# Six places of a written-out instruction order in a fused attention and MLP kernel

## The chip, the cores and the metric

The kernel runs on one core of a Trainium2 chip. The core has five engines that work through separate instruction lists: TensorE (PE in the profile, with its weight loads as PEld), VectorE (DVE), ScalarE (ACT), GpSimd (POOL) and SyncE (SP, which here only issues DMAs). They wait for each other through semaphores. The metric is the device time of one execution in microseconds; lower is better.

## The reference

Two layers, the same weights in both, act on x of shape 1 x 2048 x 512 in bfloat16:

```python
x = A_x
x = x + _A_ref(_layernorm(x, axis=-1), A_wqkv, A_wo)
x = x + _B_ref(_layernorm(x, axis=-1), B_w1, B_b1, B_w2, B_b2)
x = x + _A_ref(_layernorm(x, axis=-1), A_wqkv, A_wo)
x = x + _B_ref(_layernorm(x, axis=-1), B_w1, B_b1, B_w2, B_b2)
```

`_A_ref` is attention with 32 heads of 16 elements, where a query sees itself and the 255 keys before it: `qkv = x @ wqkv`, scores times 1/4, a softmax under that window, the sum over values, and a product with `wo`. `_B_ref` is an MLP of width 1792: `gelu(x @ w1 + b1) @ w2 + b2` with the tanh form of gelu. `_layernorm` subtracts a row's mean and divides by the root of its variance plus 1e-5.

## The kernel before

The 2048 rows are 16 tiles of 128 rows; over the two layers that makes 32 tiles (0 to 31), and 16 blocks of two tiles (0 to 15; blocks 8 to 15 are the second layer). X, all weights, the keys and values of the last blocks and the MLP's hidden rows stay in SBUF. The ten MLP jobs take two or four tiles each.

A block b runs through these steps; the name in brackets is the key of the step in the code, with b, a tile or an index behind it.

- Layer norm in front of attention (`layernorm`): statistics of a row tile on VectorE (`bs`, line 585, and `ba`, line 587), variance plus epsilon (`vp`, line 591) and the power -1/2 on POOL (`pw`, line 597), the normalised rows on VectorE (`xn`, line 607). Then a transpose: by a DMA transpose that SP issues (`tx`, line 612), or for the first four and the last tiles on TensorE (`tp`, line 619) with a copy out of PSUM (`te`, line 574 on VectorE, 576 on ACT). Numbers from 32 up belong to the layer norm in front of the MLP: `xn57` is the row tile 25 of that kind.
- Projections on TensorE, line 633: `q`, `k` (four steps of two matmuls for each half of the columns, so `q5_1.3` is block 5, second half, last step) and `v` by tile. Out of PSUM they go by `qe` (line 574 or 576), `ke` (VectorE, line 667, which also writes zeros between the heads by `parmask`) and `ve` (line 574 or 576). For each tile of V two DMAs write a copy shifted by 64 rows (`vs`, line 682).
- Attention in ten visits of a block (five in the blocks that begin a layer): scores on TensorE (`sc`, line 734), two exponentials on ACT (`ex`, line 741), 0/1 masks on VectorE or POOL (`mk`, line 762). For each half of the heads then follow the sums over values with a column of row sums (`pv`, line 784), a transpose out of PSUM (`od`, line 793), the reciprocal (`rc`, line 797), the normalisation (`nm`, line 801) and a transpose back (`ot`, line 807), all on VectorE or, for some `nm`, on POOL.
- The product with wo (`op`, line 633) and its sum into X (`rs`, line 833).
- The MLP: `m` (first product, line 633), bias on VectorE (`gb`, line 856) and gelu on ACT over two hidden chunks (`ga`, line 859), or both on ACT (`ge`, line 864); X plus b2 on POOL (`xb`, line 872); `y` (second product, 14 chunks, line 633); `ya` (line 876) adds it to X. In the second layer a tile is then stored (`out`, line 880).
- Loads: X by `ldx`, wqkv by `ldw`, w1 by `ldu`, and W2's hidden chunks in four parts, `ldz0` to `ldz3` (line 564); `ldz3` holds chunks 11 to 13.

The order of the work is written out by hand. The program adds its 3080 steps to a list, each with its engine, what it reads and writes, and the PSUM banks it takes and frees. Their numbers in the list `_ORDER` say in which order they are emitted. Each engine executes its own steps in that order. So a number that moves past steps of other engines alone changes nothing in what the engines execute. `_ALT` says which steps run on their second engine, and `_BANKS` gives the PSUM banks in the order in which they are taken.

While the steps are emitted, `_Sched.op` derives the waits: a step waits for the steps that wrote what it reads, or that still read what it writes, by the counter of their engine. DMAs use eight counters in turn, and a DMA first waits until the one eight places before it, on the same counter, has landed. SP executes its waits and issues one after the other, so that a DMA whose data are not ready holds all that stand behind it.

Of the kernel before, what the change touches and what calls it, by code (L numbers as in the profile page):

```python
# [19 lines left out]
class _Sched:  # L20
# [148 lines left out]
    61, 26, 59, 106, 20, 39, 62, 104, 28, 63, 40, 32, 64, 67, 38, 65, 107, 105, 68, 108, 66, 49, 27, 109, 69, 47, 29,  # L169
    48, 54, 5, 80, 70, 113, 81, 110, 82, 6, 114, 324, 111, 115, 71, 55, 72, 112, 73, 152, 83, 74, 126, 116, 84, 127,  # L170
    117, 128, 118, 119, 153, 150, 129, 120, 194, 130, 97, 196, 98, 31, 99, 42, 85, 195, 151, 100, 154, 366, 101, 10,
    86, 11, 367, 87, 322, 75, 103, 155, 76, 90, 521, 102, 88, 368, 91, 77, 325, 156, 78, 323, 92, 89, 79, 326, 198,
    327, 131, 199, 93, 132, 12, 94, 157, 133, 134, 200, 136, 135, 202, 137, 96, 203, 138, 139, 158, 25, 95, 121, 140,
    204, 216, 159, 201, 122, 143, 217, 144, 205, 123, 145, 197, 124, 218, 328, 146, 519, 207, 147, 125, 141, 219, 212,
    208, 213, 170, 171, 172, 214, 330, 329, 43, 370, 209, 206, 173, 210, 371, 174, 175, 160, 161, 162, 372, 163, 176,
    520, 148, 215, 177, 164, 374, 149, 373, 220, 211, 376, 331, 44, 165, 221, 166, 375, 180, 167, 168, 178, 522, 169,
    222, 379, 523, 223, 181, 524, 381, 142, 230, 225, 226, 224, 45, 231, 380, 182, 377, 179, 183, 227, 232, 184, 233,
    382, 384, 234, 185, 228, 385, 342, 229, 343, 51, 332, 378, 333, 237, 386, 187, 52, 337, 369, 334, 235, 335, 50,
    344, 238, 394, 387, 338, 396, 388, 345, 188, 236, 189, 383, 339, 346, 239, 336, 190, 240, 389, 395, 241, 527, 191,
    242, 641, 398, 347, 400, 390, 348, 340, 349, 350, 399, 352, 243, 359, 525, 244, 351, 402, 353, 403, 192, 391, 354,  # L180
    360, 341, 392, 361, 355, 404, 356, 407, 362, 409, 357, 363, 248, 249, 53, 262, 250, 263, 408, 412, 393, 193, 252,
    253, 414, 264, 528, 245, 411, 246, 254, 255, 247, 256, 410, 413, 427, 257, 526, 563, 259, 565, 397, 278, 260, 279,
    186, 261, 428, 564, 422, 416, 405, 275, 365, 276, 423, 272, 287, 281, 284, 290, 273, 566, 288, 277, 285, 282, 280,
# [5 lines left out]
    437, 537, 592, 650, 538, 556, 557, 558, 584, 593, 559, 595, 438, 651, 585, 439, 596, 652, 440, 586, 896, 597, 653,  # L189
    441, 560, 599, 587, 654, 600, 659, 660, 655, 656, 601, 588, 661, 598, 604, 589, 898, 662, 605, 456, 457, 899, 442,  # L190
    487, 458, 443, 606, 657, 444, 445, 452, 663, 453, 594, 658, 609, 446, 610, 459, 454, 466, 897, 467, 447, 449, 900,
    611, 450, 603, 607, 463, 469, 901, 478, 451, 460, 464, 612, 472, 664, 481, 461, 479, 470, 590, 468, 482, 465, 473,
# [91 lines left out]
    2300, 2581, 2291, 2284, 2285, 2301, 2484, 2580, 2304, 2562, 2302, 2485, 2305, 2292, 2286, 2294, 2287, 2572, 2486,  # L284
    2295, 2279, 2280, 2563, 2296, 2288, 2306, 2492, 2493, 2256, 2554, 2281, 2314, 2494, 2315, 2278, 2282, 2582, 2495,
    2307, 2496, 2309, 2267, 2316, 2297, 2317, 2568, 2310, 2320, 2283, 2573, 2321, 2322, 2298, 2323, 2324, 2325, 2293,
# [4 lines left out]
    2350, 2601, 2768, 2351, 2518, 2769, 2519, 2520, 2600, 2424, 2425, 2421, 2770, 2426, 2602, 2521, 2771, 2578, 2772,  # L291
    2603, 2522, 2773, 2523, 2524, 2525, 2427, 2774, 2604, 2537, 2544, 2605, 2538, 2545, 2526, 2539, 2505, 2775, 2540,
    2606, 2546, 2428, 2776, 2541, 2547, 2430, 2778, 2607, 2608, 2548, 2506, 2609, 2610, 2777, 2612, 2611, 2781, 2613,
    2543, 2782, 2614, 2617, 2780, 2615, 2354, 2504, 2355, 2618, 2616, 2356, 2783, 2357, 2786, 2619, 2371, 2422, 2787,
    2358, 2359, 2620, 2372, 2784, 2335, 2621, 2373, 2788, 2360, 2622, 2429, 2796, 2374, 2797, 2375, 2423, 2790, 2361,
    2362, 2625, 2363, 2364, 2623, 2798, 2376, 2789, 2800, 2779, 2626, 2365, 2801, 2366, 2785, 2799, 2367, 2377, 2368,
    2791, 2802, 2624, 2370, 2804, 2792, 2700, 2378, 2805, 2379, 2380, 2381, 2382, 2806, 2793, 2803, 2809, 2383, 2384,
    2810, 2654, 2794, 2385, 2655, 2643, 2656, 2811, 2657, 2807, 2814, 2658, 2644, 2815, 2645, 2812, 2646, 2649, 2813,
    2647, 2650, 2816, 2651, 2652, 2808, 2923, 2627, 2924, 2818, 2638, 2628, 2817, 2675, 2629, 2925, 2795, 2630, 2819,
# [4 lines left out]
    2833, 2703, 2704, 2834, 2752, 2753, 2705, 2836, 2933, 2706, 2707, 2708, 2835, 2837, 2709, 2710, 2932, 2838, 2839,  # L304
    2936, 2711, 2754, 2938, 2840, 2755, 2935, 2756, 2934, 2757, 2841, 2712, 2937, 2713, 2714, 2758, 2715, 2941, 1971,
    2759, 2942, 2842, 2760, 2751, 2550, 2761, 2762, 2735, 2943, 2542, 2763, 2951, 1954, 2736, 2952, 2737, 2944, 2764,
    2843, 2765, 2738, 2766, 2739, 2953, 2740, 2955, 2939, 2549, 2718, 2940, 2957, 2945, 2741, 2742, 2743, 2744, 2956,
    2745, 2746, 2747, 2748, 2719, 2749, 2958, 2720, 2959, 2946, 2750, 2961, 2906, 2767, 2960, 2847, 2947, 2851, 2848,
    2963, 2852, 2721, 2854, 2853, 2969, 2954, 2722, 2971, 2962, 2855, 2849, 2723, 2861, 2948, 2724, 2970, 2725, 2856,
    2949, 2844, 2726, 2727, 2845, 2972, 2964, 2973, 2728, 2846, 2966, 2729, 2950, 2730, 2862, 2731, 2965, 2863, 2880,  # L310
    2865, 2732, 2858, 2881, 2866, 2968, 2733, 2859, 2967, 2984, 2860, 2979, 2352, 2974, 2386, 2850, 2857, 2907, 2975,
# [636 lines left out]
```

## Time and profile before

| | |
|---|---|
| time, median of 3 runs | 460.92 us (460.57 to 461.63) |
| profiled execution, its own time | 459.81 us |
| its span | 458.0 us, mean granted TensorE clock 0.992 |
| TensorE busy | 421.5 us (92%) |
| weight loads | 230.7 us (50%) |
| VectorE busy | 345.7 us (75%) |
| ScalarE busy | 389.7 us (85%) |
| POOL busy | 201.3 us (44%) |
| share of the chain that ended last | PE 60%, ACT 17%, DVE 13%, DMA 4%, SP 2% |

The busy shares are means over the whole span; matmuls are pipelined, so a busy TensorE is not one at its peak. The chain is followed back from the last instruction: at each step to what released it, or to the instruction before it on its engine. In a timeline, a line gives the start in us from the span's start, the duration, engine, line and operation, what it writes and reads, shapes, how many instructions were joined, and in brackets the idle time before it with what ended it.

These DMA issues are the ones that the change moves or moves past (start of the issue, its duration, and landing where the trace has one, in us):

| step | issue | lasts | landed |
|---|---|---|---|
| vs6_0 | 43.46 | 0.47 | |
| ldz3 | 43.98 | 0.58 | 49.55 |
| vs5_1 | 44.62 | 0.53 | 49.75 |
| tx9 | 45.19 | 3.45 | 50.93 |
| tx8 | 48.69 | 1.26 | 51.53 |
| vs4_1 | 49.99 | 0.73 | 52.24 |
| out1 | 414.11 | 0.58 | 416.06 |
| vs31_1 | 414.74 | 0.47 | 416.88 |
| vs30_0 | 415.25 | 0.60 | 417.33 |
| out0 | 415.88 | 0.59 | 419.81 |
| tx61 | 416.51 | 2.55 | 420.33 |
| vs31_0 | 419.11 | 0.58 | |

### The profile page before, as it was taken

The page shows a single profiled execution, that of the slowest core. Times are in us where ns is not written, and L with a number is a line of the kernel's source. Part 1 is how long each engine was busy: PE and PEld are TensorE (multiplying, and loading weights), DVE is VectorE, ACT ScalarE, POOL GpSimd, SP SyncE. Part 2 cuts the span into 40 slices and gives each one's busy share as a digit, 9 for nine tenths or more (in the row PEclk, how much of TensorE's full clock was granted, in tenths as well). Part 3 has the DMA queues.
Part 4 walks back from the last instruction along what each step waited for, and adds up shares of the span by engine and source line. Part 5 has one row for each costly group of instructions (what it writes and reads, how often), then busy time and mean ns, then how long its engine had stood idle before and what let it go on. Part 6 is the DMA issues. An engine that isn't in the chain of part 4 may idle for free.

```text
span 458.0 us, 16828 instructions
## 1 busy us (share of the span) xinstructions
PE 421.5 (92%) x7505; PEld 230.7 (50%) x7579; DVE 345.7 (75%) x640; ACT 389.7 (85%) x463; POOL 201.3 (44%) x225
## 2 busy tenths in 40 slices
PE   7998999986789997899999998999999999999996
PEld 4555646543434553445445454455554554444573
DVE  6999699787773878986698688857987497755762
ACT  2998979988799999789999988999889988898642
POOL 4272614054336145351855563564652444524230
PEclk9999999998899999999999999999999999999999
DMA  8687311202300103210032022010422003003110
GB/s 236 192 216 171 71 32 26 43 9 35 82 4 1 24 15 66 58 26 0 3 61 44 0 59 35 10 43 1 74 45 53 1 4 89 3 1 91 36 47 24
DMA packets 47972, 23.25 MB, mean 51 GB/s; under 512 B 33180, under 2 KB 47900, under 8 KB 47900
## 3 DMA queue, kind: packets, MB, share of 16 engines
q1 hardware_dynamic: 47900, 22.17, 21.8%
q8 instruction: 60, 0.98, 1.0%
q14 instruction: 12, 0.10, 0.1%
HBM read 8.00 MB, written 2.10 MB: 22 GB/s over the span
## 4 chain that ended last, share of the span: by engine, by line
PE 60%; ACT 17%; DVE 13%; DMA 4%; issue 3%; SPq 2%; POOL 1%; DVEq 0%
PE ps L633 44%; ACT E L741 11%; PE ps L784 8%; PE ps L734 8%; ACT gT L864 3%; DVE E L762 2%; DVE OD L793 2%; ACT gT L859 2%; DMA xnTB<-xn 2%; DVE xn L607 2%; DVE gT L856 1%; DMA xnTA<-xn 1%; DVE Va L574 1%; DVE OT L807 1%; DVE X L876 1%
## 5 line engine op out<-in xcount | busy, mean ns | idle before, releaser
L741 ACT ACTIVATE E<-ps 128x1024 bf16<-128x1024 f32 x300 | 283.8, 1035 | 40.1 <-PE ps L734 39.4
L762 POOL TENSOR_TENSOR E<-E,mask 128x512 bf16<-128x512 bf16 (+2 forms) x104 | 114.6, 1115 | 100.4 <-ACT E L741 100.1
L633 PE MATMUL ps<-xnTB,W_sb 128*128 128x512 bf16 (+1 forms) x541 | 110.8, 336 | 4.9 <-issue 1.4
L633 PE MATMUL ps<-W_sb,gT 128*128 128x512 bf16 x418 | 110.9, 380 | 3.8 <-issue 2.5
L633 PE MATMUL ps<-xnTA,Wqkv_sb 128*128 128x256 bf16 x512 | 75.2, 274 | 2.3 <-DMA xnTA<-xn 1.2
L633 PEld LDWEIGHTS ps<-xnTB,W_sb 128*128 128x128 bf16 x560 | 51.3, 98 | 47.9 <-issue 5.5
L762 DVE TENSOR_TENSOR E<-E,mask 128x768 bf16<-128x768 bf16 (+2 forms) x132 | 63.5, 498 | 10.7 <-ACT E L741 10.6
L734 PE MATMUL ps<-QT,KT 32*128 32x128 bf16 (+3 forms) x1920 | 61.5, 232 | 10.7 <-ACT E L741 3.9
L734 PEld LDWEIGHTS ps<-QT,KT 32*128 32x128 bf16 x1920 | 28.9, 93 | 64.2 <-ACT E L741 38.5
L633 PEld LDWEIGHTS ps<-W_sb,gT 128*128 128x128 bf16 x448 | 39.9, 98 | 40.5 <-issue 2.7
L793 DVE STREAM_TRANSPOSE OD<-ps 128x1024 f32<-128x1024 f32 x32 | 39.8, 1244 | 25.9 <-PE ps L784 25.8
L633 PEld LDWEIGHTS ps<-xnTA,Wqkv_sb 128*128 128x128 bf16 x512 | 46.3, 98 | 25.7 <-issue 5.5
L864 ACT ACTIVATE gT<-ps,b1T 128x512 bf16<-128x512 f32 (+1 forms) x80 | 43.4, 610 | 11.5 <-PE ps L633 11.4
L784 PE MATMUL ps<-E,Va 64*17 64x128 bf16 (+3 forms) x1920 | 44.2, 233 | 4.6 <-DVE E L762 1.9
L801 POOL TENSOR_TENSOR Nb<-OD,Rc 128x512 bf16<-128x512 f32 x17 | 18.3, 1076 | 64.4 <-DVE Rc L797 64.4
L667 DVE TENSOR_TENSOR KT<-ps,parmask 128x1024 bf16<-128x1024 f32 x32 | 38.7, 1210 | 10.2 <-PE ps L633 9.9
L872 POOL TENSOR_TENSOR Xb<-X,b2all 128x512 f32<-128x512 bf16 x32 | 37.9, 1193 | 19.1 <-DVE X L876 11.7
L856 DVE TENSOR_SCALAR gT<-ps,b1T 128x512 bf16<-128x512 f32 (+1 forms) x60 | 37.3, 632 | 11.4 <-PE ps L633 10.3
L784 PE MATMUL ps<-E,Vs 64*17 64x128 bf16 (+3 forms) x1920 | 44.9, 233 | 0.0
L585 DVE BATCH_NORM_STATS2 stat<-X 128x6 f32<-128x512 bf16 x64 | 42.6, 679 | 2.9 <-DMA X<-in_A_x_dram 2.5
L784 PEld LDWEIGHTS ps<-E,Va 64*17 64x17 bf16 x1920 | 37.2, 85 | 14.0 <-issue 9.0
L633 PE MATMUL ps<-Wo_sb,OT 128*128 128x512 bf16 x118 | 37.4, 387 | 2.8 <-DVE E L762 1.2
(51 smaller groups left out, 363.1 us busy)
## 6 DMA issues: line engine op xcount, KB each, us to landing
Vs<-Va SPq DMA_DIRECT2D x64, 68.0 KB, 2.5
W_sb<-in_B_w_dram SPq DMA_DIRECT2D x4, 512.0 KB, 6.0
out_dram<-X SPq DMA_DIRECT2D x16, 128.0 KB, 1.9
X<-in_A_x_dram SPq DMA_DIRECT2D x3, 512.0 KB, 6.3
Wqkv_sb<-in_A_wqkv_dram SPq DMA_DIRECT2D x4, 256.0 KB, 6.0
W_sb<-in_B_w_dram SPq DMA_DIRECT2D x1, 768.0 KB, 5.8
W_sb<-in_B_w_dram SPq DMA_DIRECT2D x2, 384.0 KB, 5.1
Wqkv_sb<-in_A_wqkv_dram SPq DMA_DIRECT2D x1, 512.0 KB, 7.0
```

Of the source, the lines that this page charges most:

```text
L585: add("dve", lambda e, B, t=t, k6=k6: e.bn_stats(stat6[:, k6, :], X[:, t, :]), reads=["X%d" % t], writes=["st%d" % k6], key="bs%d" % (k + j))
L633: r = e.matmul(ps[:, B[g][0], cols], lhsT, rhs, start=st, stop=sp)
L667: add("dve", lambda e, B, g=g, i=i: e.tensor_tensor(out=KT[:, kb, 2 * i : 2 * i + 2].rearrange("p c m a q -> p a (c m) q"), in0=ps[:, B[g] ...
L734: x = e.matmul(ps[:, bk[r], o : o + n], KT[rows, kb, c, m].rearrange("p a q -> p (a q)"), QT[rows, c, q : q + n], start=True, stop=True)
L741: add("act", lambda e, B, g_=g_, gi=gi: e.activation(E[:, 2 * gi : 2 * gi + 2, e0 : e0 + 512], ps[:, B[g_][0] : B[g_][0] + 2, :], AF.Exp, ...
L762: fn = lambda e, B: e.tensor_tensor(out=Ew, in0=Ew, in1=Mw, op=ALU.mult)
L784: x = e.matmul(ps[32 * r : 32 * r + VW, B[g][par], c % 2 * 2 * P + lo : c % 2 * 2 * P + hi], V[rows, (2 * b + m // 2) % VR, c * HC + 2 * r ...
L793: add("dve", lambda e, B: e.transpose(OD[:, s].rearrange("p a c q -> p (a c q)"), ps[:, B[g][0] : B[g][0] + 2, :]), reads=["ps:" + g], wri ...
L801: return e.tensor_tensor(out=Nb[:, s, :].rearrange("p (k a d) -> p a k d", a=2, d=Dh), in0=sums[:, :, :, 0:Dh], in1=rc[:, :, :, None].to_b ...
L856: add("dve", lambda e, B, g=g, fc=fc: e.tensor_scalar(out=gT[:, fc, c0 : c0 + M], in0=ps[:, B[g][0], 0:M], scalar1=b1T[:, fc : fc + 1], sc ...
L864: add("act", lambda e, B, g=g, fc=fc: e.activation(gT[:, fc, c0 : c0 + M], ps[:, B[g][0], 0:M], AF.Gelu_apprx_tanh, bias=b1T[:, fc : fc + ...
L872: add("pool", lambda e, B, t=t, xs=xs: e.tensor_tensor(out=Xb[:, xs, :], in0=X[:, t, :], in1=b2all[:], op=ALU.add), reads=["X%d" % t, "b2a ...
```

## The change

Only `_ORDER` differs. Most of the numbers that move there pass steps of other engines alone. Read engine by engine, ACT and POOL execute the same lists as before, the PSUM banks are taken in the same order, and this is what differs:

- VectorE, at the start: the list `bs7, te2, bs5, ke0_0, ba5, bs4, ke1_0, ba4` (numbers 324, 112, 152, 84, 153, 150, 130, 151) becomes `te2, bs7, ke0_0, bs5, ba5, ke1_0, bs4, ba4`. So the copy of a transposed row tile and the first key evictions of blocks 0 and 1 stand in front of a statistic each.
- SP: `ldz3, vs5_1, tx9, tx8` (53, 193, 528, 526) becomes `vs5_1, tx9, tx8, ldz3`.
- TensorE: `q5_1.3` (657) goes in front of `m1_4.0, m1_4.1, m1_0.0, m1_0.1` (456, 457, 442, 443).
- VectorE: `xn57, ot13_1` (2505, 2606) becomes `ot13_1, xn57`; the transpose of block 13's output stands in front of the normalised rows of tile 25.
- SP: `out1, vs31_1, vs30_0, out0, tx61, vs31_0` (1971, 2550, 2542, 1954, 2843, 2549) becomes `vs31_1, vs30_0, tx61, vs31_0, out1, out0`.

The eight DMA counters go by place, so the DMAs in the two stretches of SP change counters among themselves.

```diff
...
-    48, 54, 5, 80, 70, 113, 81, 110, 82, 6, 114, 324, 111, 115, 71, 55, 72, 112, 73, 152, 83, 74, 126, 116, 84, 127,
-    117, 128, 118, 119, 153, 150, 129, 120, 194, 130, 97, 196, 98, 31, 99, 42, 85, 195, 151, 100, 154, 366, 101, 10,
+    48, 54, 5, 80, 70, 113, 81, 110, 82, 6, 114, 111, 115, 71, 55, 72, 112, 324, 73, 83, 84, 74, 126, 116, 152, 127,
+    117, 128, 118, 42, 119, 153, 129, 130, 150, 120, 194, 97, 196, 98, 31, 99, 85, 195, 151, 100, 154, 366, 101, 10,
...
-    360, 341, 392, 361, 355, 404, 356, 407, 362, 409, 357, 363, 248, 249, 53, 262, 250, 263, 408, 412, 393, 193, 252,
-    253, 414, 264, 528, 245, 411, 246, 254, 255, 247, 256, 410, 413, 427, 257, 526, 563, 259, 565, 397, 278, 260, 279,
+    360, 341, 392, 361, 355, 404, 356, 407, 362, 409, 357, 363, 248, 249, 262, 250, 263, 408, 412, 393, 193, 252, 253,
+    414, 264, 528, 245, 411, 246, 254, 255, 247, 256, 410, 413, 427, 257, 526, 563, 259, 565, 397, 278, 260, 53, 279,
...
-    441, 560, 599, 587, 654, 600, 659, 660, 655, 656, 601, 588, 661, 598, 604, 589, 898, 662, 605, 456, 457, 899, 442,
-    487, 458, 443, 606, 657, 444, 445, 452, 663, 453, 594, 658, 609, 446, 610, 459, 454, 466, 897, 467, 447, 449, 900,
+    441, 560, 599, 587, 654, 600, 659, 660, 655, 656, 601, 588, 661, 598, 604, 589, 898, 662, 605, 657, 456, 457, 899,
+    442, 487, 458, 443, 606, 444, 445, 452, 663, 453, 594, 658, 609, 446, 610, 459, 454, 466, 897, 467, 447, 449, 900,
...
-    2603, 2522, 2773, 2523, 2524, 2525, 2427, 2774, 2604, 2537, 2544, 2605, 2538, 2545, 2526, 2539, 2505, 2775, 2540,
-    2606, 2546, 2428, 2776, 2541, 2547, 2430, 2778, 2607, 2608, 2548, 2506, 2609, 2610, 2777, 2612, 2611, 2781, 2613,
+    2603, 2522, 2773, 2523, 2524, 2525, 2427, 2774, 2604, 2537, 2544, 2605, 2538, 2545, 2526, 2539, 2606, 2505, 2775,
+    2540, 2546, 2428, 2776, 2541, 2547, 2430, 2778, 2607, 2608, 2548, 2506, 2609, 2610, 2777, 2612, 2611, 2781, 2613,
...
-    2936, 2711, 2754, 2938, 2840, 2755, 2935, 2756, 2934, 2757, 2841, 2712, 2937, 2713, 2714, 2758, 2715, 2941, 1971,
-    2759, 2942, 2842, 2760, 2751, 2550, 2761, 2762, 2735, 2943, 2542, 2763, 2951, 1954, 2736, 2952, 2737, 2944, 2764,
-    2843, 2765, 2738, 2766, 2739, 2953, 2740, 2955, 2939, 2549, 2718, 2940, 2957, 2945, 2741, 2742, 2743, 2744, 2956,
+    2936, 2711, 2754, 2938, 2840, 2755, 2935, 2756, 2934, 2757, 2841, 2712, 2937, 2713, 2714, 2758, 2715, 2941, 2759,
+    2942, 2842, 2760, 2751, 2550, 2761, 2762, 2735, 2943, 2542, 2763, 2951, 2736, 2952, 2737, 2944, 2764, 2843, 2765,
+    2738, 2766, 2739, 2953, 2740, 2955, 2939, 2549, 2718, 2940, 1971, 2957, 1954, 2945, 2741, 2742, 2743, 2744, 2956,
...
```

18 rows, old and new, of the table _ORDER are left out of this document.

## The prediction

> **What bounds the kernel now.** I read the page first (engines, chain), then the chain in order of time, then the timeline of each engine around the six places. All durations are from the one profiled execution: span 458.0, its own time 459.81, so 1.8 lie around the span. The median of the three runs is 460.92, 1.1 above it; the sum is made against 459.81 and carried over to the median as a difference. The three runs lie between 460.57 and 461.63, so about 0.2% (0.92 us) is what a measurement can tell from no change.
>
> ```profile
> PE 421.5 (92%) x7505; PEld 230.7 (50%) x7579; DVE 345.7 (75%) x640; ACT 389.7 (85%) x463; POOL 201.3 (44%) x225
> PE 60%; ACT 17%; DVE 13%; DMA 4%; issue 3%; SPq 2%; POOL 1%; DVEq 0%
> ```
> The chain changes engine every few microseconds: all engines run fixed lists and hand work to each other. Nothing but the first loads from HBM has a time of its own, so a microsecond won on the chain is kept to the end, unless a neighbour that was almost as late takes over. Each place is therefore worked out up to the next such neighbour.
>
> ```profile
> 9.40 0.69 DVE L585 BATCH_NORM_STATS2 stat<-X 128x6 f32<-128x512 bf16 x1 [0.81 <-DMA X<-in_A_x_dram]
> 10.02 0.41 DVE L574 COPY xnTA<-ps 128x512 bf16<-128x512 bf16 x1
> 10.48 1.92 PE L633 MATMUL ps<-xnTA,Wqkv_sb 128*128 128x256 bf16 x16 [0.32 <-DVE xnTA L574]
> ```
> At the start VectorE sits idle until rows 4 to 7 of X land, does a statistic, and only then the copy (te2) that TensorE waits for.
>
> ```profile
> 43.98 0.58 SPq L564 DMA_DIRECT2D W_sb<-in_B_w_dram  x1
> 44.62 0.53 SPq L682 DMA_DIRECT2D Vs<-Va  x1
> 45.19 3.45 SPq L612 DMA_TRANSPOSE xnTA<-xn  x1
> 51.58 1.26 PE L633 MATMUL ps<-xnTA,Wqkv_sb 128*128 128x256 bf16 x10 [0.67 <-DMA xnTA<-xn]
> ```
> SP issues W2's last part (ldz3), a shifted copy of V (vs5_1), then transpose tx9, whose issue lasts 3.45 where the median of its kind is 1.26; TensorE waits 0.67 for the pair.
>
> ```profile
> 376.55 0.69 DVE Nb L801
> 377.25 1.29 DVE xn L607
> 378.54 0.62 DVE OT L807
> 379.16 1.19 DVE Va L574 x2
> ```
> That is the chain through block 13: normalisation of the output (nm13_1), xn57, transpose ot13_1, then ve30 and ve31. The POOL row that overlaps is
>
> ```profile
> 377.24 1.15 POOL L762 TENSOR_TENSOR E<-E,mask 128x512 bf16<-128x512 bf16 x1 [1.96 <-ACT E L741]
> ```
> and at the end
>
> ```profile
> 416.51 2.55 SPq L612 DMA_TRANSPOSE xnTB<-xn  x1
> 419.11 0.58 SPq L682 DMA_DIRECT2D Vs<-Va  x1
> 421.41 0.28 PE L784 MATMUL ps<-E,Va 64*17 64x256 bf16 x4 [0.33 <-DMA Vs<-Va]
> ```
> where pv15_0 waits 0.33 for vs31_0, issued last behind two stores, two copies and a slow transpose.
>
> **The change part by part.** Nothing is added or removed. ACT's and POOL's lists stay as they are; TensorE's changes by one step, VectorE's by four, SP's by three.
>
> *VectorE's start.* Before: bs7, te2, bs5, ke0_0, ba5, bs4, ke1_0, ba4. After: te2, bs7, ke0_0, bs5, ba5, ke1_0, bs4, ba4. te2's input is ready at 9.30 (the chain's last transpose ends there), so it starts at 9.34 instead of 10.02 and ends at 9.75. TensorE is then busy until 9.88 with its weight loads and goes on with k1 at 9.89 instead of 10.48: 0.59 earlier. ke0_0 starts at 9.34 + 0.32 + 0.62 = 10.28 (issue distances of te2 and bs7 in the rows), against 10.94; its input ends near 10.2. sc0_0 then follows k1's 16 matmuls and goes out 0.6 earlier, as does ACT's first exponential (12.78 to about 12.19). But VectorE itself has the same work: the list from 9.40 to ve1 lasts 4.54, and two pairs bs, ba now stand back to back, which costs 0.09 each (0.68 from start to start at 51.45, against 0.58 to 0.60 with something between). So ve1 may start at 9.34 + 4.54 + 0.18 = 14.06 instead of 14.17, and ve0, with the 0.12 that it waited for TensorE gone, at 17.45 instead of 17.68. Scores sc0_2 wait for ve0; ACT's chain behind them gains 0.25 to 0.29. The statistics lose nothing: ba4, which starts POOL's rstd, ends at 14.0 as before, and xn4 has 1.2 to spare before its transpose. Taken: -0.25, nearest to the VectorE rows, which bind. Ends: 0 and -0.6 (TensorE's row).
>
> *q5_1.3 on TensorE* goes in front of m1_4.0. Two matmuls, 0.21 at 75.56, move into a wait of 0.84 (73.92 to 74.76, for transpose tx35). The chain runs from m1_4.1 to VectorE (gb1_4 at 75.43), ahead of the old place, so this is worth 0; end -0.2.
>
> *W2's last part on SP* goes behind vs5_1, tx9, tx8. With 0.58 + 0.05 gone, tx9 is issued at about 44.55, and if it takes 1.26, tx8 goes out at 45.85 to 47.1 and lands near 48.7 instead of 51.53 (1.6 after its issue ended, as now). Even with a second transpose of 2.3, as elsewhere in this trace, it lands by 50. TensorE wants the pair at 50.8: m0_11.1 has left and the first gelu (ge0_9) has freed its bank at 50.74. k4 then starts at 50.82 instead of 51.58; y1.4 waits for ACT's ga0_4, done at 53.75, and goes at 53.80 instead of 54.53; pv1_1, VectorE's od1_1 and the scores behind it follow 0.7 earlier, ACT's next exponential too (it had 1.35 idle). ldz3 is issued near 47.2, and 5.6 from issue to landing as now gives 52.8; its first reader y1.11 comes at 58.6. vs4_1 and vs7_1 are issued earlier than now, and their readers (70.2 and later) are far. Each DMA also waits for the one eight places before it on its counter; the counters turn by one for four transfers, all these predecessors have landed by 40.64 (at the tail by 390). Taken: -0.70 (the wait of 0.67 plus the issue step). Ends: 0, if the 3.45 is not ldz3's doing, and -0.77.
>
> *ot13_1 in front of xn57.* xn57 takes 1.38 where the median is 0.41: POOL's mask runs 377.24 to 378.39, and xn57 ends 0.15 behind it at 378.54. After: ot13_1 377.16 to 377.87 (it and nm show no stretching in any of their rows), xn57 from 377.78, again held by the same mask to 378.54. ve30 starts at 378.46 instead of 379.09: 0.63 earlier; with it ve31, sc14_3 and ACT. op26.2 on TensorE starts at 378.6 instead of 379.21. The next neighbour is SP: tx57 goes out as before (378.72), so vs28_1 still lands at 386.82, and pv14_0 starts at 386.87 instead of 387.33. Taken: -0.46. Ends: -0.63, and +0.1 if xn57 is stretched once more from its later start (tx57 0.6 later, vs28_1 with it).
> The Trainium skill, page "SBUF — State Buffer", section "Who interferes with whom", says that VectorE's fast modes and GpSimd take one port pair as a lock and that whichever starts second waits until the first is through. Here xn57 starts at 377.16, 0.08 ahead of the mask, and is the one that waits; so the trace agrees that one waits, not with who. By a full wait xn57 would run 378.39 to 378.80, tx57 0.26 later, and this place would give -0.2 and the sum -1.45, still inside the forecast's case below.
>
> *Two stores on SP* go behind vs31_0. out1 and out0 take 0.58 + 0.59 of issue and some of tx61's 2.55. After: vs31_1, vs30_0, tx61 from 415.25, vs31_0 at 416.6 to 417.9, landed by 420. The stores follow by 419.2, before out10 (421.07), and nobody reads them. TensorE has sc15_7 until 421.05, so pv15_0 goes at 421.1 instead of 421.4. Taken: -0.30. Ends: 0 and -0.33.
>
> Sum: -0.25 + 0 - 0.70 - 0.46 - 0.30 = -1.7. Profiled execution 458.1, median 459.2.
>
> **The rivals.**
> 1. *The slow issue is not the load's.* Among the DMA packets one of 16 KB of instructions starts near 45.0 as well and takes 2.3, and transposes are slow without any load near: SP's tx12 at 84.29 takes 2.11. If tx9 stays slow for that reason, the third term falls away: -1.0, median 459.9. Against it: 3.45 is the longest of all 58 transposes, and the only one with a load just ahead.
> 2. *The gains are hidden.* VectorE at the start keeps its work, PE's 0.67 and 0.33 are waits of which the neighbour takes over at once. Then -0.3 at most: 460.6. For it: VectorE's own 4.54. Against it: ge0_9 is ready 0.8 ahead of the transposes, and sc15_7 0.3 ahead of vs31_0.
> 3. *Slower: VectorE against POOL.* POOL and VectorE share the masks of all blocks. Where they meet, one is stretched: mk1_7_0 took 1.84 and mk2_0_0 1.37 (the pair at 48.30 is 3.13) where 0.42 and 0.53 are clean; xn57 lost 0.97. The change shifts VectorE and TensorE by 0.2 to 0.7 against ACT and POOL at four places. The place where it hurts is the stretch of VectorE alone on the chain, masks mk2_8_0 to mk2_7_0 at 78.3 to 81.4, beside POOL's mk2_7_1: there the earlier q5_1.3 brings ACT's exponentials, and so the masks, forward by up to 0.2 against POOL. From three stretched operations on (2.9) the sum is positive: +1.2, median 462.1. Against it: after 55.07 POOL is idle until 63.7, so the largest shift meets nobody.
>
> **How the numbers follow.** The forecast, -1.7 with 0.5 either way, has 0.60. Rival 1 has 0.17 (half of it beyond 0.2%), rival 2 0.11, rival 3 0.12. Faster: 0.60 + 0.08 = 0.68. Within 0.2%: 0.09 + 0.11 = 0.20. Slower: 0.12. The range goes down to 458.2 (all the negative ends together give -2.5, of which a little lies below) and up to 461.2 (rival 2 with the scatter of the runs). The likeliest case alone spans 458.5 to 460.0.
>
> **What would show it.** te2 ahead of bs7 and TensorE's k1 near 9.9; ACT's first exponential near 12.2 and ve0 near 17.45; tx9's issue back at 1.2 to 1.3 and k4 without a DMA wait; ot13_1 at 0.6 ahead and ve30 right behind xn57; pv15_0 without its wait for Vs. Wrong would be: tx9 or tx8 still above 2.5, a wait of y1 for W2, or masks over 0.9 us on the chain that were short before.

## The result and the profile after

| | before | after |
|---|---|---|
| median, first comparison (22 runs each) | 460.86 us | 458.87 us, ratio 0.9963 (95%: 0.9947 to 0.998) |
| median, second comparison (29 and 12 runs) | 460.40 us | 459.43 us, ratio 0.9978 (0.9955 to 1.0) |
| profiled execution, its own time | 459.81 us | 458.49 us |
| its span | 458.0 us | 456.8 us |

The change makes the kernel faster by 0.2 to 0.4%, by the ratios 1.7 us in the first comparison (0.9 to 2.4) and 1.0 us in the second, where the interval (0 to 2.1) just reaches no change. One of the 29 runs was in a slower state of the chip and is left out of the ratio. The prediction said 459.2 us and -1.7. The lines below answer those that it showed. First the page of the changed kernel, the engines' busy time and the chain:

```profile
PE 422.9 (93%) x7505; PEld 231.1 (51%) x7579; DVE 345.3 (76%) x640; ACT 389.8 (85%) x463; POOL 201.1 (44%) x225
PE 65%; ACT 18%; DVE 13%; issue 3%; DMA 1%; DVEq 0%
```
The work is the same. The chain's 4% of DMA and 2% of SP's queue have become 1% and none. Part of that is the change: tx9's slow issue with the landing behind it, and vs31_0, are off the chain. But the first load of X and two transposes at 20.38 and 173.04, where nothing was changed, have left it as well, so the shares alone don't measure the change.

VectorE's timeline at the start (start, duration, engine, line, shapes, in brackets the idle time before it):

```profile
10.04 0.42 DVE L574 COPY xnTA<-ps 128x512 bf16<-128x512 bf16 x1 [0.94 <-PE ps L619]
10.38 0.68 DVE L585 BATCH_NORM_STATS2 stat<-X 128x6 f32<-128x512 bf16 x1
10.98 1.21 DVE L667 TENSOR_TENSOR KT<-ps,parmask 128x1024 bf16<-128x1024 f32 x1
```
te2 is now first and waits for TensorE's transpose alone. It is no earlier than before (10.02), because tp2, the transpose ahead of it, began 0.71 later in this execution. Ahead of the first transposes TensorE runs 14 warm-up matmuls (line 526), whose results nobody reads, and these took longer. TensorE's timeline of before and then of the changed kernel:

```profile
1.24 4.49 PE L526 MATMUL ps<-gT 128*128 128x512 bf16 x14 [1.24 <-DVE gT L524]
```
```profile
1.24 6.08 PE L526 MATMUL ps<-gT 128*128 128x512 bf16 x14 [1.24 <-DVE gT L524]
```
The trace's record of the granted clock begins with full clock at 3.90 us in before and at 7.13 here; a warm-up matmul takes some 0.63 ahead of that time and 0.38 behind it. TensorE's list is the same up to here in both kernels. Of the 14 profiled executions of this study that of before reached full clock first, and this one last (with loads_early_again).

SP's queue around W2's last part, and TensorE's first key matmuls behind the transposes:

```profile
45.54 3.34 SPq L612 DMA_TRANSPOSE xnTA<-xn  x2
48.92 0.59 SPq L564 DMA_DIRECT2D W_sb<-in_B_w_dram  x1
51.81 1.25 PE L633 MATMUL ps<-xnTA,Wqkv_sb 128*128 128x256 bf16 x10
```
The bracket with 0.67 of DMA wait is gone from k4. But the two issues take 3.34, which is 2.03 for tx9 and 1.27 for tx8; tx9 is not back at 1.26.

VectorE through block 13, and POOL's mask beside it:

```profile
376.30 0.69 DVE L801 TENSOR_TENSOR Nb<-OD,Rc 128x512 bf16<-128x512 f32 x1
377.02 0.71 DVE L807 STREAM_TRANSPOSE OT<-Nb 128x512 bf16<-128x512 bf16 x1
377.66 0.63 DVE L607 TENSOR_SCALAR xn<-X,statmv,rstd 128x512 bf16<-128x512 bf16 x1
378.21 1.28 DVE L574 CAST Va<-ps 128x512 bf16<-128x512 f32 x2
```
```profile
376.99 1.16 POOL L762 TENSOR_TENSOR E<-E,mask 128x512 bf16<-128x512 bf16 x1 [1.95 <-ACT E L741]
```
ot13_1 follows nm13_1, and xn57 lasts 0.63 instead of 1.38: it starts 0.50 later and ends again 0.14 behind the mask.

SP's queue and TensorE's sums at the end:

```profile
414.73 1.22 SPq L612 DMA_TRANSPOSE xnTB<-xn  x1
415.99 0.59 SPq L682 DMA_DIRECT2D Vs<-Va  x1
416.62 1.70 SPq L880 DMA_DIRECT2D out_dram<-X  x2
420.31 0.28 PE L784 MATMUL ps<-E,Va 64*17 64x256 bf16 x4
```
vs31_0 goes out 3.1 us earlier and pv15_0 has no wait.

**How the places are measured.** Two executions of one kernel differ by more than a place is worth, so a place can't be read from a difference of times. But a stretch between two steps, one ahead of a place and one behind it, has the same length in every execution in which the same thing limits it. This table gives such stretches in us, from the profiled executions of all kernels of this study ("moved" has the change at that place, "not" has the order of before there; an execution in which something else was altered inside the stretch is left out of that row):

| place, from start of to start of | not moved, each execution | mean | moved, each execution | mean | worth |
|---|---|---|---|---|---|
| start: tp2 to ex0_2_0 | 10.14 10.21 10.26 9.69 9.65 9.65 9.65 | 9.89 | 9.93 to 9.94 (six) | 9.94 | +0.05 |
| W2's last part: m0_11.1 to ge0_7 | 5.72 5.67 5.64 5.53 5.50 | 5.61 | 5.01 to 5.04 (seven) | 5.01 | -0.60 |
| ot13_1: ex14_1_1 to ex15_2_0 | 35.41 to 35.45 (six) | 35.42 | 34.97 34.96 35.21 34.84 35.23 34.96 35.05 | 35.03 | -0.39 |
| two stores: sc15_7 to od15_0 | 2.20 1.98 1.93 1.89 1.81 1.81 1.81 | 1.92 | 1.81 (seven) | 1.81 | -0.11 |

The first number of each "not" list is the execution of the kernel before that the prediction was worked out from. The sum of the last column is -1.05 us, or 0.23%; q5_1.3 adds nothing that can be read. Both measured intervals hold it. The sum takes it that gains at different places add up, and that all of a stretch's gain reaches the end.

### The profile page after: what moved, and what is told of

Its sections match the earlier page's. It is cut to its first block, busy times and chain, and to the rows that moved or that the text cites. A ratio compares the mean times of both kernels' runs of the same rounds, so it can differ in the third digit from the quotient of the medians.

```text
span 456.8 us, 16828 instructions
## 1 busy us (share of the span) xinstructions
PE 422.9 (93%) x7505; PEld 231.1 (51%) x7579; DVE 345.3 (76%) x640; ACT 389.8 (85%) x463; POOL 201.1 (44%) x225
## 4 chain that ended last, share of the span: by engine, by line
PE 65%; ACT 18%; DVE 13%; issue 3%; DMA 1%; DVEq 0%
PE ps L633 47%; ACT E L741 11%; PE ps L734 8%; PE ps L784 7%; ACT gT L864 3%; DVE OD L793 2%; ACT gT L859 2%; DVE E L762 2%; DVE gT L856 2%; PE ps L526 1%; DVE KT L667 1%; DVE stat L585 1%; DVE OT L807 1%; DMA xnTB<-xn 1%; DVE xn L607 1%
```

## One place at a time

Each kernel is the one before with one place of the change. The diffs give the steps in the order of the engine concerned.

**only_start**

```diff
 VectorE:
-bs7, te2, bs5, ke0_0, ba5, bs4, ke1_0, ba4
+te2, bs7, ke0_0, bs5, ba5, ke1_0, bs4, ba4
```


> The kernel before with VectorE's start alone in the new order (te2, bs7, ke0_0, bs5, ba5, ke1_0, bs4, ba4). Read as shifts: how far a step starts from where it started in the profile before, behind the place minus ahead of it. The loads' landings differ between executions, so tp2, ahead of the place, is the reference. My account: TensorE's k1_0.0 about -0.6 against tp2, but ACT's ex0_2_0 only about -0.25, because VectorE's own list binds at ve0; time 460.6 for 460.9. Rival, that the wait was hidden: k1_0.0 moves, ex0_2_0 does not (0.0), time the same. Second rival, that statistics put behind the evictions delay rstd on POOL (vp4): ex0_2_0 +0.3 or more against tp2.

Measured: ratio 0.9981 (0.9957 to 1.0004). In its profile te2 follows tp2 by 0.48 (1.16 before), k1 is 0.58 earlier against tp2, ve0 0.19 and ex0_2_0 0.20. Read against the one execution of before this is what was forecast (0.59 and 0.25). The table shows why it is not a gain. VectorE's timeline in an execution with the old order (the kernel mask_dve, below, which is the same there):

```profile
8.65 0.69 DVE L585 BATCH_NORM_STATS2 stat<-X 128x6 f32<-128x512 bf16 x1 [0.21 <-DMA X<-in_A_x_dram]
9.26 0.41 DVE L574 COPY xnTA<-ps 128x512 bf16<-128x512 bf16 x1
9.59 0.68 DVE L585 BATCH_NORM_STATS2 stat<-X 128x6 f32<-128x512 bf16 x1
```
Here rows 4 to 7 of X landed at 8.63, 0.06 ahead of the start of tp2 (8.69), where in the kernel before they landed 0.53 behind it. The statistic bs7 then filled time in which VectorE would have waited for TensorE, and te2 starts 0.57 after tp2, only 0.09 later than with the change. With the change bs7's 0.6 comes behind te2, in front of the key evictions: from te2 to ex0_2_0 it takes 9.46 instead of 8.97 to 9.08. So the move wins 0.2 to 0.3 where these rows land 0.5 to 0.65 behind tp2 (three executions), and loses 0.25 to 0.3 where they land with it (four). With the change the stretch no longer depends on them: it is 9.93 to 9.94 where they land 0.05 ahead and where they land 0.39 behind. Both sides of this distance vary over the 14 executions. The rows land between 8.63 and 9.89, and tp2 begins between 8.69 and 9.56, mostly late where the warm-up matmuls last long. They took 4.49 in the execution of before, 5.73 to 5.96 in three of the four where the rows land with tp2; in the fourth, mask_dve, the rows were early.

**only_ldz3**

```diff
 SyncE:
-ldz3, vs5_1, tx9, tx8
+vs5_1, tx9, tx8, ldz3
```


> The kernel before with W2's last part alone put behind the transposes tx9 and tx8. My account: k4_0.0 loses its wait for the transposes, and the shift between m0_11.1 (ahead) and ACT's ge0_7 and ex2_1_1 (behind) is -0.7; y1.11 does not wait for W2. Rival, that the slow tx9 is not the load's doing: tx9's issue stays above 3 and the shift is 0. Rival, that the gain is hidden: the transposes land before 49.5, but the shift is above -0.2. Time -0.7 against before.

Measured: ratio 0.9966 (0.9943 to 0.999). The stretch over the place is 5.01 instead of 5.72, a gain of 0.71. tx9's issue took 2.31. SP's queue in this kernel:

```profile
45.48 3.62 SPq L612 DMA_TRANSPOSE xnTA<-xn  x2
49.15 0.58 SPq L564 DMA_DIRECT2D W_sb<-in_B_w_dram  x1
```
Against the execution that the term was worked out from it is confirmed, and tx9's issue is still nearly twice the usual.

**only_ot13**

```diff
 VectorE:
-xn57, ot13_1
+ot13_1, xn57
```


> The kernel before with ot13_1 alone put in front of xn57. My account: xn57 starts 0.5 to 0.6 later against its neighbours but ends where it ended (held by POOL's mask), ve30 shifts by -0.63, sc14_3 and ACT's ex14_3_0 by -0.6, and pv14_0 by -0.46 to -0.6, where vs28_1 comes next. Rival, a full lock from xn57's new start: xn57 ends 0.26 later and ve30 shifts by -0.37. Rival, hidden: ACT's ex14_7_0 shifts by less than 0.2. Time -0.5 against before.

Measured: ratio 0.9986 (0.9963 to 1.001). ve30 comes 0.62 earlier against the steps ahead of the place, pv14_0 0.59, ex15_2_0 0.44. The place holds.

**only_stores**

```diff
 SyncE:
-out1, vs31_1, vs30_0, out0, tx61, vs31_0
+vs31_1, vs30_0, tx61, vs31_0, out1, out0
```


> The kernel before with the two stores alone put behind vs31_0. My account: tx61's issue falls from 2.55 to about 1.3, vs31_0 is issued 2 to 3 earlier, pv15_0 loses its wait of 0.33 and od15_0 and all behind it shift by -0.3. Rival, hidden: od15_0 shifts by less than 0.1 because something else is as late as vs31_0. Time -0.3 against before.

Measured: ratio 0.9992 (0.9966 to 1.0018). The stretch over the place is 1.81 instead of 2.20, which looks like a gain of 0.39. But it is 1.81 in only_start and in only_ot13 too, where the stores stand in the old place: tx61's issue took 2.17 and 2.04 there, 2.55 in the profile of before, and vs31_0 then landed in time. The wait of 0.33 was that of one execution; in the six others with the stores in the old place the stretch is longer than 1.81 by 0.17 at most, and on average the place gives 0.11.

The four ratios together say -0.75%, more than the whole change, with about 0.25% of uncertainty each. They can't rank the places; the stretches can.

## What holds tx9 up

**small_z** is the kernel before with other parts of W2, so that ldz3, still ahead of tx9, has a third of its bytes:

```diff
-W2_CUTS = ((0, 4), (4, 8), (8, 11), (11, 14))
+W2_CUTS = ((0, 4), (4, 8), (8, 13), (13, 14))
```


> The kernel before, its order unchanged, but W2 is cut at chunk 13 instead of 11, so that ldz3 holds one chunk (128 KB) instead of three (384 KB) and ldz2 five instead of three. ldz3 still goes out just ahead of vs5_1 and tx9. Theory A (the bytes of ldz3 hold up the transpose behind it): tx9's issue falls from 2.9 to 3.6 (the four executions where ldz3 is ahead) to 1.9 to 2.4, about what it is where ldz3 stands behind (2.03 and 2.31), and k4_0.0 shifts by -0.5 to -0.7 across the place. Theory B (rival 1 of the prediction: the fetch of instructions that runs beside it): tx9's issue stays at 2.9 to 3.6 and k4's wait for the transposes at 0.5 to 0.7. The 5-chunk ldz2 should leave the rest alone, or lengthen the stall at sc1_7 (0.97 to 2.33 so far) by some tenths.

Measured: 459.89 us in one run. tx9's issue took 2.60, between the two theories, and k4 had no wait (5.01 over the place). SP's queue:

```profile
45.19 0.58 SPq L564 DMA_DIRECT2D W_sb<-in_B_w_dram  x1
45.82 0.47 SPq L682 DMA_DIRECT2D Vs<-Va  x1
46.33 3.90 SPq L612 DMA_TRANSPOSE xnTA<-xn  x2
```
So bytes matter, and they are not all of it.

**w2_three_early** is the kernel before with the other three parts of W2 sent out earlier, in time that SP spends waiting for data (from 29.0 to 32.5 in before); ldz3 stays ahead of tx9 with all its bytes:

```diff
 SyncE:
-ldu2, vs4_0, ldz1, ldz2, ldz0, tx32
+ldu2, ldz1, ldz2, ldz0, vs4_0, tx32
```


> The kernel before with only ldz1, ldz2, ldz0 early; ldz3 still ahead of vs5_1 and tx9. This tells whose work the slow issue of tx9 is. If the load ldz3 alone holds it: tx9's issue stays near 2.4 to 3.5 and k4 waits 0.4 to 0.7 for the transposes. If it needs the fetch of instructions beside it, which the early loads pull away from it: 1.2 to 2.0 and no wait. sc1_7 0.2 to 0.3 as in loads_early.

Measured: 457.81 us in one run, and tx9 and tx8 issue in 2.58 together, 1.28 for tx9:

```profile
43.55 1.23 SPq L564 DMA_DIRECT2D W_sb<-in_B_w_dram  x1
44.84 0.48 SPq L682 DMA_DIRECT2D Vs<-Va  x1
45.37 2.58 SPq L612 DMA_TRANSPOSE xnTA<-xn  x2
```
The load alone, then, does not hold tx9. What does is seen in the DMA view of the stretch of tx9's issue. Before (45.2 to 48.6), queues by packets, MB and share:

```profile
q1 hardware_dynamic: 464, 0.45, 44.6%
q8 instruction: 1, 0.02, 4.2%
```
and w2_three_early (45.3 to 46.7):

```profile
q1 hardware_dynamic: 263, 0.27, 60.5%
```
The second has more traffic for its length (0.27 MB in 1.4 us against 0.45 in 3.4) and no packet of instructions. In before that packet (16 KB, from 45.30) takes 2.29 and the issue 3.45; in w2_three_early it ran from 43.11 to 44.41, over before tx9, and it is ldz3's own issue that lasts 1.23 instead of 0.58. Over the 14 profiled executions of this study (812 transposes) there is no exception: every one of the 171 transposes whose issue took over 1.4 us overlapped a packet of queue 8, and none of the 569 that met no such packet took over 1.4.

The load's part is the length of the packet: 1.81 to 2.49 in the five executions with all of ldz3 ahead of tx9, 1.43 with a third of it, 1.07 to 1.34 with ldz3 behind. In all nine tx9's issue is the packet's time plus 0.96 to 1.17, as if SP stood still while the packet is under way. (Over all 171 it is the packet's time plus 0.3 to 1.4, 0.8 in the middle.) So rival 1 named the right cause of the slow issue, but it priced it wrongly: the packet without the load beside it is 0.8 us shorter on average (1.22 against 2.06), and that, with the issue slot of 0.63, is enough for the transposes to come in time.

## What holds xn57 up

**mask_dve** is the kernel before, with the mask that runs beside xn57 on the other engine:

```diff
-mk14_1_0 on POOL
+mk14_1_0 on VectorE, behind bs58
```


> The kernel before, but the mask mk14_1_0 is computed by VectorE, behind bs58, instead of by POOL beside xn57. Theory A (POOL's mask stretches xn57): xn57 takes 0.41 instead of 1.38, ot13_1 starts at its end, and ve30 shifts by -0.97 against the steps before the place; it is 0.35 better there than moving ot13_1 ahead was (-0.62, -0.63). Behind bs58 VectorE then has 0.55 more to do. Theory B (xn57 waits for something else, such as the write of its rows): xn57 stays above 1.0.

Measured: 460.77 us in one run. xn57 takes 0.41 and ve30 comes 0.97 earlier against ex14_1_1, as theory A said:

```profile
377.64 0.69 DVE L801 TENSOR_TENSOR Nb<-OD,Rc 128x512 bf16<-128x512 f32 x1
378.25 0.41 DVE L607 TENSOR_SCALAR xn<-X,statmv,rstd 128x512 bf16<-128x512 bf16 x1
378.57 0.70 DVE L807 STREAM_TRANSPOSE OT<-Nb 128x512 bf16<-128x512 bf16 x1
```
It is POOL's mask that stretches xn57. But the gain is lost by pv14_0, 0.38 later than in before, and by the mechanism of rival 3. Three masks of VectorE, joined in one line, and POOL's mask that they now meet:

```profile
386.45 2.05 DVE L762 TENSOR_TENSOR E<-E,mask 128x768 bf16<-128x768 bf16 x3
```
```profile
386.90 1.45 POOL L762 TENSOR_TENSOR E<-E,mask 128x512 bf16<-128x512 bf16 x1 [1.81 <-ACT E L741]
```
The last of the three (mk14_3_1) takes 1.24 where it took 0.28 in the changed kernel, and pv14_0 waits for it. The changed kernel was spared this meeting, but not every one. Two masks of one visit, mk14_8_0 on VectorE and mk14_8_1 on POOL, start together at about 393, and ot13_1's move shifts VectorE there by 0.2 to 0.6 against ex14_1_1. VectorE's mask in before, then in the changed kernel, and POOL's row in the changed kernel, where mk14_8_1 is the second of the two joined and runs from 392.60 to 393.26:

```profile
393.39 0.41 DVE L762 TENSOR_TENSOR E<-E,mask 128x512 bf16<-128x512 bf16 x1
```
```profile
392.62 0.93 DVE L762 TENSOR_TENSOR E<-E,mask 128x512 bf16<-128x512 bf16 x1
```
```profile
391.49 1.77 POOL L762 TENSOR_TENSOR E<-E,mask 128x512 bf16<-128x512 bf16 x2
```
In the seven executions where VectorE's mask starts ahead, by 0.02 to 0.07, it takes 0.41 to 0.42 and POOL's 0.88 to 0.92. In six POOL's starts ahead, by 0.02 to 0.18, and in one the two start within 0.01; in these VectorE's takes 0.77 to 0.97 and POOL's 0.66 to 0.68. Here, then, the one that starts first goes through and the other is stretched. Six of the seven executions with ot13_1 ahead are among these, and none of the six with the old order in this place. So such a meeting lengthens an operation by 0.4 to 1.0; what it costs the kernel depends on what waits for it, which is much less at this place (see the account of ot13_1 below).

## Further on: the loads and the statistics

TensorE has a stall of its own at sc1_7, near 40. The timeline of before and then of the changed kernel; "issue" means that the profile shows nothing it waited for:

```profile
40.30 0.25 PE L734 MATMUL ps<-QT,KT 32*128 32x192 bf16 x1 [0.31 <-ACT E L741]
41.07 0.40 PE L734 MATMUL ps<-QT,KT 32*128 32x192 bf16 x11 [0.52 <-issue]
```
```profile
40.80 0.25 PE L734 MATMUL ps<-QT,KT 32*128 32x192 bf16 x1 [0.31 <-ACT E L741]
42.00 0.40 PE L734 MATMUL ps<-QT,KT 32*128 32x192 bf16 x11 [0.95 <-issue]
```
sc1_7 took 0.97 and 1.40 here, and up to 2.33 in the other executions. The stall comes behind the step's first matmul, and a step's waits for other engines all stand ahead of it. A packet of 16 KB of instructions ends 1.5 to 1.8 us before each of these stalls does, while three parts of W2 fill the queues.

**loads_early** and **loads_early_again** (one kernel, run twice) are the changed kernel with these three parts ahead of vs4_0, as in w2_three_early.

> The changed kernel, and W2's parts ldz1, ldz2, ldz0 go out right behind ldu2, ahead of vs4_0, for which SP waits some 3.4 us; so they are issued at about 29.6 to 31.3 instead of 33.5 to 35.2. Theory A (the fetch of instructions that TensorE waits for at sc1_7 is slow because these loads fill the DMA engines): the loads have landed by 38, before the fetch starts (38.6 to 40.1 in six executions), sc1_7 lasts 0.9 or less instead of 0.97 to 2.33, and the time is 0.4 to 1.0 below that of the changed kernel (ratio to the kernel before 0.994 to 0.9955). Theory B (the fetch takes that long by itself): sc1_7 still lasts 1.0 to 2.3, and the ratio stays at that of the change, 0.9963 within 0.001. A third way, slower: the loads now meet tx7 and the copies of V at 28 to 33, and tx7's issue or landing goes over 2.5.

> The changed kernel with ldz1, ldz2, ldz0 right behind ldu2, once more. Theory A (the stall of TensorE at sc1_7, which took 0.97 to 2.33 in nine executions and 0.20 with these loads early, is really gone, and nothing behind takes the gain): median 0.8 to 1.5 below that of the changed kernel in the same comparison, ratio 0.993 to 0.995. Theory B (it is taken back in the stretch 110 to 130, where the granted clock drops to 0.5 for some microseconds in each execution, at another place each time): median within 0.4 of the changed kernel.

**change_again** is the changed kernel in the same comparison as loads_early_again.

> The changed kernel itself, beside the next two, since differences of 0.2% between runs made at different times are too fine to be told. Expected from the sum of the places (-0.2, -0.7, -0.5 and 0 for the stores): ratio 0.9965 to 0.997. At the stores, sc15_7 to od15_0 shifts by -0.39 as in every execution but that of the kernel before, moved or not.

Measured: loads_early 457.67 us, ratio to before 0.9965 (0.9941 to 0.999); loads_early_again 457.76 us, 0.9938 (0.9914 to 0.9961), beside change_again 459.43 us, 0.9978 (0.9955 to 1.0). The stall is gone in both:

```profile
40.09 0.40 PE L734 MATMUL ps<-QT,KT 32*128 32x192 bf16 x12 [0.31 <-ACT E L741]
```
sc1_7 takes 0.20, and ACT's next exponential (ex1_7_1) comes 0.77 earlier than in before, counted from ex1_6_0 ahead of it (1.19 earlier than in the changed kernel). tx9 is back at 1.26 and 1.27, since the next packet too comes earlier now and ends 0.4 us ahead of tx9. The packet ahead of sc1_7 isn't shorter than with the loads beside it (1.17 to 1.18 against 1.07 to 1.14); it starts earlier, 2.4 to 2.5 ahead of sc1_7 instead of 0.6 to 1.7. Counted from the scores ahead (sc1_6) it starts between 0.1 ahead and level, where it started 0.7 to 1.9 behind. So theory A was right in that the loads are the cause, and wrong in how: with them the packet comes later, not longer. Nor had the loads landed by 38, ahead of the packet: the last of the three landed at 38.94 and 40.09, 0.2 and 0.5 behind its end. Why the packet comes later with them is not shown. By the medians this kernel beats the changed one by 1.7 us in the same comparison; in the run before, where the changed kernel did not run beside it, its ratio (0.9965) was no better than the change's had been (0.9963). So it is probably the fastest of the study, by an amount that isn't settled.

**w2_all_early** sends out ldz3 as well, right behind ldz0.

> As loads_early_again, and ldz3 too goes behind ldz0, so that all of W2 is issued by 32.0. By theory A sc1_7 stays at 0.2 to 0.3 if the last load has landed by about 38.6 (384 KB more, at the some 160 to 200 KB per us that these loads have shown: about 2 us later than with three), tx9 stays at 1.2 to 1.3, and the time is that of loads_early_again within 0.3. By theory B no difference from the changed kernel. Slower than loads_early_again if the load is still under way when the fetch starts.

Measured: 458.84 us, ratio 0.9965 (0.9948 to 0.9982). sc1_7 took 1.17 again. The packet began at 38.82, 0.6 behind sc1_6, and ldz3 landed at 40.91, 0.9 behind the packet's end. That is the last way of the expectation, a load still under way; that the number of bytes decides it is likely, but one execution doesn't show it. tx9 took 1.27, tx8 1.89, for now the second packet fell on tx8.

**stats_late** puts VectorE's later statistics behind the first masks in the changed kernel:

```diff
 VectorE (changed kernel):
-te2, bs7, ke0_0, ... ve1, bs6, bs9, ba7, xn4, ba6, ke0_1, ve0, ... mk0_0_0, xn6, bs8, ve3
+te2, ke0_0, ... ve1, xn4, ke0_1, ve0, ... mk0_0_0, bs7, ba7, bs6, ba6, ve3, od0_0, xn6, xn7, bs9, bs8
```


> The changed kernel, and on VectorE the statistics bs7, ba7, bs6, ba6, bs9, bs8 of the later row tiles, and xn6, go behind the first masks (with the POOL steps vp6 and pw6 and the transpose tx6 behind them). Theory A (from te2 on it is VectorE's own list that limits the start, which is why the early copy brings 0.2 and not 0.59): ke0_0 to ve0 is 2.3 shorter in work, so ke0_1 and ve0 start as soon as TensorE has their inputs, ve0 by 0.5 to 1.2 earlier against tp2, and ex0_2_0 by 0.4 to 1.0; the time is 0.4 to 0.9 below that of the changed kernel if the later transposes tx6 and tx7 are not needed earlier. Theory B (ACT's exponentials limit): ex0_2_0 gains less than 0.2. A third way, slower: tx6 and tx7, now 2 to 4 later, hold up TensorE's projections of block 3 at 25 to 32, and what is won at 15 is lost there.

Measured: 463.41 us, ratio 1.0083 (1.0055 to 1.011): slower. With some 2 us of work out of its way, VectorE brings ex0_2_0 only 0.18 nearer to tp2 (9.75 instead of 9.93). VectorE's timeline shows the next neighbour:

```profile
16.19 0.42 DVE L607 TENSOR_SCALAR xn<-X,statmv,rstd 128x512 bf16<-128x512 bf16 x1 [1.09 <-POOL rstd L597]
16.53 1.20 DVE L667 TENSOR_TENSOR KT<-ps,parmask 128x1024 bf16<-128x1024 f32 x1
```
xn4 waits for POOL's power (pw4), two initialisation steps of POOL behind ba4, and the key eviction ke0_1 stands behind xn4. So theory A falls: VectorE's list is the limit, but POOL's chain from ba4 is only 0.2 behind.

The time is lost later, and not in the third way. The transposes tx6 and tx7 are issued 3.6 and 2.4 us later than in the changed kernel, but TensorE has no wait for a DMA between 14 and 60. It waits for VectorE, whose statistics now stand in front of the key eviction ke2_0 that the scores sc1_2 need. VectorE's timeline (xn6 and xn7, bs9 and bs8, ke2_0), and TensorE's wait:

```profile
25.09 1.53 DVE L607 TENSOR_SCALAR xn<-X,statmv,rstd 128x512 bf16<-128x512 bf16 x2
26.55 1.27 DVE L585 BATCH_NORM_STATS2 stat<-X 128x6 f32<-128x512 bf16 x2
28.41 1.20 DVE L667 TENSOR_TENSOR KT<-ps,parmask 128x1024 bf16<-128x1024 f32 x1
```
```profile
29.76 0.40 PE L734 MATMUL ps<-QT,KT 32*128 32x192 bf16 x12 [2.28 <-DVE statmv L587]
```
ke2_0 ran at 25.91 in the changed kernel. Besides the two statistics, xn6 takes 1.21 instead of 0.41 beside a mask of POOL and ends 0.15 behind it, as xn57 did; and the mask mk0_3_0, behind ke2_0, takes 1.16 instead of 0.39, for which pv0_1 waits 0.68.

## Why the prediction was right, and where it was not

The range (458.2 to 461.2) holds both medians of the changed kernel, 458.87 and 459.43 lie on both sides of the forecast of 459.2, and "faster" was right. That the first comparison gave the forecast's 1.7 is in part luck: the places, measured over many executions, account for 1.05, and the second comparison gave 1.0. Step by step:

- **The start, -0.25.** The working of the one execution was right: te2 0.48 behind tp2, k1 0.58 earlier, ve0 0.19 and the exponential behind it 0.20. The term was not: over seven executions with the old order and six with the new the place is worth +0.05. The step that failed is the first, "te2's input is ready at 9.30 ... instead of 10.02": it took the landing of X's rows 4 to 7, 0.53 behind tp2, for a fixed number. It varied from 0.06 ahead of tp2 to 0.65 behind it. Part of this is tp2 itself, which comes behind the warm-up matmuls, and these were shortest of all in the execution of before. "The statistics lose nothing: ba4 ... ends at 14.0 as before" was wrong by 0.18 to 0.19.
- **q5_1.3, 0.** Right. ex2_9_1 comes 0.14 earlier against gb1_4 in all five executions looked at, and 0.03 of it is left at ge1_10.
- **W2's last part, -0.70.** The profiled pair gives -0.70 and only_ldz3 -0.71. Against the mean of five executions with the old order it is -0.60, because k4's wait was 0.67 in the execution of before and less in the others. "If it takes 1.26" was wrong: tx9 took 2.0 to 2.3 in the three executions with ldz3 behind it and the other loads in their old place, the packet of instructions having stayed. tx8 landed at 50.09 instead of near 48.7, in an execution that is 0.9 later by then (at m0_11.1), so it kept the second bound ("lands by 50"); k4 started at 51.8 and didn't wait.
- **ot13_1, -0.46.** ve30 moved by 0.62 to 0.63 in seven executions (0.63 forecast). pv14_0 moved by 0.24 to 0.59, on average by 0.46, which is the forecast; and the neighbour named for it, vs28_1, is the one that binds in five of the seven (pv14_0 starts 0.06 after it lands). The mean further on, at ex15_2_0, is -0.39: where mk14_8_0 is stretched, 0.05 to 0.14 of the gain at pv14_0 is gone by then, and 0.01 where it is not (loads_early). The other reading, a full wait by the page "SBUF — State Buffer" of the Trainium skill (section "Who interferes with whom"), is not what the trace shows: xn57 now starts 0.67 behind the mask and ends 0.14 behind it, not 0.4. Whether the part of xn57 that moves data waits in full is not shown.
- **The stores, -0.30.** Mis-sized: -0.11 on average. The step that failed is the neighbour: "sc15_7 [is ready] 0.3 ahead of vs31_0" held in the execution of before and in none of the six others with the old order: the stretch is 1.81, that is without the wait, in three of them and 0.08 to 0.17 longer in the other three.
- **Rivals.** Rival 1 was right about the packet and wrong that the gain hangs on it. Rival 2 (gains hidden) was half right at the start and at the stores. Rival 3 occurred, at another place than the one named and at a far smaller price: mk14_8_0 on the chain took 0.93 (0.77 in the second execution) instead of 0.42, which costs 0.05 to 0.14 and not the stretch itself. The masks mk2_8_0 to mk2_7_0, where it was feared, took what they took before.
- **The range.** That of the -2.5 of all the negative ends "a little lies below" 458.2 is a slip: 460.92 less 2.5 is 458.4, inside the range.

The sum of the averages, -1.05, is a little under two thirds of the forecast. All four large terms were waits that stood out in one execution, and in each of the four the other executions with the old order had shorter ones on average or the same. The profile pair itself differs by only 1.2 in span, because other things went against the changed kernel in that execution: the longer warm-up of TensorE (tp2 +0.71) and the stall at sc1_7 (+0.43). What remains open: whether moving te2 also steadies the stall at sc1_7, which took 1.29, 1.30 and 1.40 in the three executions with the move alone and the loads in their old place, 1.73 in stats_late, where te2 is ahead too, and 0.97 to 2.33 in six without the move. That is too few to say.

## What to carry to other kernels

A wait picked from one profile because it stands out is likely to be shorter in the next execution (it was at three of the four places here), so a term should be the mean over several executions, and a place is measured by the distance between a step ahead of it and a step behind it, not by the total. Before working from a profile's first microseconds, see how long the warm-up took in it and in others. An idle time ahead of a late input may be filled with work in the order as it stands; moving the critical step ahead then only trades places with that work, and who wins is decided by which input lands first. Where a DMA's issue is slow, look for packets of instructions in that stretch before blaming the load beside it, and send large loads out in SP's idle time, well ahead of such packets.

## What the runs showed of the hardware

- A packet of 16 KB of instructions holds up what SP issues at that time: a transpose's issue of 1.2 to 1.3 us becomes the packet's time plus 0.3 to 1.4 (0.96 to 1.17 at tx9). All 171 issues of transposes over 1.4 us in 14 executions met one.
- TensorE stalls with the same packets. With loads of W2 under way it stood 0.5 to 1.8 us in the middle of one group of scores (sc1_7) in eleven executions, with nothing shown as the releaser, each time until 1.5 to 1.8 us behind the end of a packet; in the three with three loads sent out early it did not.
- The granted clock of TensorE falls to 0.5 for 3.4 or 6.8 us at a time (less where the span ends). One such stretch or two lie between 110 and 131 us in each of the 14 executions, but not at the same step, and most have one elsewhere too (102.9 in before, 106.1 in the changed kernel). Windows of 3 us of before, and then of the changed kernel (busy time, clock, DMA share, GB/s):

```profile
119.00:122.00 3.00, 2.35 (x24) 1.00 0.36 81
122.00:125.00 3.00, 1.90 (x128) 0.73 0.40 81
```
```profile
116.00:119.00 3.00, 2.80 (x40) 0.56 0.42 91
119.00:122.00 3.00, 2.95 (x24) 0.87 0.22 49
```
  From ex4_0_0 to ex4_5_0, some 13 us in this stretch, it takes 14.06 to 14.99 in the five executions with 6.8 us of half clock there and 12.53 to 13.41 in the nine others (12.74 in before). This scatter is as large as the whole change.
- VectorE and POOL on masks and normalisation at the same time: xn57 takes 0.41 alone, 0.63 when it starts 0.67 behind a mask of 1.16, and 1.38 when it starts 0.08 ahead of one; it ended 0.14 to 0.15 behind the mask in the last two. Of the masks mk14_8_0 and mk14_8_1, which start within 0.2 of each other, the first to start takes its usual time and the other is stretched, in 13 of 14 executions; in the other they start within 0.01.
- The full clock of TensorE is first recorded between 3.90 and 7.13 us from the span's start, though the warm-up matmuls begin at 1.24 in every execution; the 14 of them take 4.49 to 6.08.
